# First rows loaded as bf16 over the hardware queues, weight columns ahead, and normalisation scalars read directly, in a two-layer transformer kernel

## The chip, the cores and the metric

The kernel runs on one core of a Trainium2 chip. The metric is device time in microseconds (us): the median of several executions. Experiments of one group ran on the same chip, in turns with the kernel before.

The engines are PE (matmuls), ACT (activation functions), DVE (elementwise work), POOL (slower elementwise work and one kind of DMA) and SP (issues DMAs). Each engine works through its own instruction list.

## The reference

Two rounds of attention and a gated MLP, with the same weights in both rounds. S = 2048 rows, D = 512, 32 heads of 16, F = 1792, all bf16.

```python
def _layernorm(x, axis=-1, eps=1e-5):
    m = jnp.mean(x, axis=axis, keepdims=True)
    v = jnp.var(x, axis=axis, keepdims=True)
    return (x - m) / jnp.sqrt(v + eps)
...
    x = A_x
    x = x + _A_ref(_layernorm(x, axis=-1), A_wqkv, A_wo)
    x = x + _B_ref(_layernorm(x, axis=-1), B_w_gate, B_w_up, B_w_down)
    x = x + _A_ref(_layernorm(x, axis=-1), A_wqkv, A_wo)
    x = x + _B_ref(_layernorm(x, axis=-1), B_w_gate, B_w_up, B_w_down)
```

`_A_ref` is softmax attention over all 2048 keys, and `_B_ref` is `(gelu(x@wg) * (x@wu)) @ wd`.

## The kernel before

Rows are handled in four blocks of 512 rows. The "head" is the start of the program: X is loaded, normalised and transposed to XNT block by block, and K, Q and V are projected from XNT. Attention works in units (four heads for one block of queries). A unit makes score groups on PE, exponentials on ACT (some on DVE), and P·V on PE. After the eight units of a query block, a "post" runs beside the next block's attention: output projection, normalisation, MLP, normalisation.

The order on each engine is fixed when the program is generated. The generator keeps a clock of its own, gives every operation an assumed cost, and always emits what it believes to be ready next. The last number of each operation below is that assumed cost in us.

```python
    def ln_scale(n, then):
        ...
        job("pool", 1, [
            (lambda e: e.tensor_scalar(LNS[:, 0, 0:n], var, LN_EPS, None, op0=ALU.add), mvk, [("LNS",)], 0.3),
            (lambda e: e.tensor_tensor(LNS[:, 1, 0:n], LNS[:, 0, 0:n], CM05[:, 0:n], op=ALU.pow),
             [("LNS",), ("CM05",)], [("LNS",)], 1.1),
            (lambda e: e.tensor_scalar(LNS[:, 2, 0:n], mean, -1.0, None, op0=ALU.mult), mvk + [("LNS",)], [("LNS",)],
             0.3)], then)

    def ln_apply(i, xs_, eng, alt, then=None):
        job(eng, 1, [(lambda e: e.tensor_scalar(xn(i, alt), X[:, xs_, :], LNS[:, 2, i:i + 1], LNS[:, 1, i:i + 1],
                                                op0=ALU.add, op1=ALU.mult),
                      [("X", xs_), ("LNS",)], [xnkey(i, alt)], 1.05 if eng == "pool" else 0.46)], then)
...
    def post(layer, qb):            # cut
        ...
        yield from ln_thread(tts, xsl, True, (layer, qb, 2), "dve" if qb == NQB - 1 else "pool")
        ...                          # MLP, cut
        if not last:
            yield from ln_thread(tts, xsl, True, (layer, qb, 1), "dve" if qb == NQB - 1 else "pool")
```

PE takes "keep-clock" matmuls (zeros added to the accumulator, L1253) when it would otherwise idle. They are meant to keep its clock up.

## Time and profile before

| | before |
|---|---|
| time, median of 3 | 1768.59 us |
| ACT busy | 1602 us, 91% |
| PE busy (keep-clock included) | 1614 us, 91% |
| DVE busy | 1276 us, 72% |
| POOL busy | 208 us, 12% |

The timeline of ACT in the first 100 us of the kernel before. Columns: start, busy us, engine, line, operation, out<-in, count, and in brackets the idle time before and what ended it. Instructions that follow each other are merged.

```profile
0.79 1.28 ACT L561 ACT_TABLE_LOAD   x1 [0.79 <-PEq L2260]
18.56 0.60 ACT L561 ACTIVATE fXNT<-fPS 128x512 bf16<-128x512 bf16 x1 [16.49 <-PE fPS L552]
...
30.78 6.82 ACT L1128 ACTIVATE fPT<-fPS 128x1536 bf16<-128x1536 f32 x5 [9.03 <-PE fPS L1123]
50.14 6.86 ACT L1128 ACTIVATE fPT<-fPS 128x1536 bf16<-128x1536 f32 x5 [12.54 <-PE fPS L1123]
60.92 8.16 ACT L1128 ACTIVATE fPT<-fPS 128x1536 bf16<-128x1536 f32 x6 [3.92 <-PE fPS L1123]
74.96 25.64 ACT L1128 ACTIVATE fPT<-fPS 128x1536 bf16<-128x1536 f32 x26 [5.87 <-PE fPS L1123]
```

The first exponentials start at 30.8 us. They come in bursts of five or six, because unit 0 needs the K of each further key block. From 75 us on ACT runs without long gaps. Of PE's 1614 us, 257 us are keep-clock matmuls, so ACT is the engine with the most real work, and its idle time before 75 us is what a faster head can recover.

The normalisation applies in the same kernel (query by source line: minimum, median and maximum duration in ns, first and last start):

```profile
L545 POOL TENSOR_SCALAR fHT<-fX,fLNS x36: 768/772/777, 294.9 to 1548.7; 128x512 bf16<-128x512 f32 x36
L545 DVE TENSOR_SCALAR fHT<-fX,fLNS x28: 528/541/3620, 14.2 to 1720.9; 128x512 bf16<-128x512 f32 x28
```

### The profile page before, as it was taken

The numbers are of one execution on the slowest core, as the hardware profiler recorded it, in microseconds if no ns is written. First come the engines' busy times: TensorE is split into PE (matmuls) and PEld (weight loads), VectorE is DVE, ScalarE is ACT, GpSimd is POOL, SyncE is SP. The second block draws the span as 40 slices with busy tenths as digits, with TensorE's granted clock in tenths as the row PEclk, the third lists the DMA queues.
The fourth block names the chain that finished last, engine by engine and source line by source line (L and its number), as shares of the span: only waits on it lengthen the run. The fifth ranks groups of instructions, "written<-read, shape, count | busy, mean of one in ns | idle before, by whom it ended". The sixth has DMA issues, their size and how long they took to land.

```text
span 1766.0 us, 38383 instructions
## 1 busy us (share of the span) xinstructions
PE 1614.0 (91%) x16180; PEld 497.5 (28%) x16349; DVE 1276.4 (72%) x2103; ACT 1602.1 (91%) x1488; POOL 208.2 (12%) x226
## 2 busy tenths in 40 slices
PE   7898989999899999989999989999989899999998
PEld 3422222222222222332333322222222222222233
DVE  5799996577856878538653799767895588856853
ACT  2699889999999999999899999999999999999932
POOL 2502011011110011010330110201011000101000
PEclk9999999999999999999999999999999999999999
DMA  5200000143111530125214100013401142012513
GB/s 156 73 2 17 2 15 10 47 119 115 41 37 41 162 86 17 43 57 158 65 48 133 41 18 9 17 49 102 148 18 31 51 134 91 23 39 81 152 27 104
DMA packets 138705, 114.00 MB, mean 65 GB/s; under 512 B 12320, under 2 KB 126240, under 8 KB 138528
## 3 DMA queue, kind: packets, MB, share of 16 engines
q1 hardware_dynamic: 134256, 103.07, 20.3%
q0 software_dynamic: 4272, 8.39, 1.7%
q8 instruction: 133, 2.18, 0.5%
q14 instruction: 44, 0.36, 0.1%
HBM read 97.78 MB, written 6.82 MB: 59 GB/s over the span
## 4 chain that ended last, share of the span: by engine, by line
ACT 61%; PE 21%; DVE 14%; issue 1%; POOL 1%; DMA 1%; SPq 0%; DVEq 0%; POOLq 0%
ACT fPT L1128 58%; DVE fPI L1162 6%; PE fPS L575 6%; PE fPS L1123 5%; DVE fPP L1184 5%; PE fPS L1233 4%; PE fPS L1253 3%; ACT fHT L1094 2%; PE fPS L932 2%; DVE fQ L618 1%; PE fPS L638 1%; DVE fHT L545 1%; ACT L1094 1%; DMA fX<-in_A_x_dram 0%; POOL fVD L651 0%
## 5 line engine op out<-in xcount | busy, mean ns | idle before, releaser
L1128 ACT ACTIVATE fPT<-fPS 128x1024 bf16<-128x1024 f32 (+1 forms) x1440 | 1527.4, 1212 | 83.1 <-PE fPS L1123 81.1
L1123 PE MATMUL fPS<-fQ,fKT 32*128 32x512 bf16 x4096 | 554.2, 385 | 71.5 <-ACT fPT L1128 56.0
L1162 DVE TENSOR_SCALAR fPI<-fPS 128x512 int16<-128x512 f32 x768 | 504.3, 683 | 65.5 <-PE fPS L1123 63.9
L1233 PE MATMUL fPS<-fPT,fVP 128*17 128x512 bf16 x3328 | 432.9, 384 | 13.1 <-ACT fPT L1128 6.7
L1184 DVE TENSOR_SCALAR fPP<-fPI 128x2048 int16<-128x2048 int16 x576 | 393.7, 716 | 4.4 <-PE fPS L1233 3.4
L1123 PEld LDWEIGHTS fPS<-fQ,fKT 32*128 32x128 bf16 x4096 | 138.8, 91 | 617.3 <-ACT fPT L1128 527.1
L1233 PE MATMUL fPS<-fPP,fVD 128*17 128x512 f16 x2304 | 302.3, 381 | 6.4 <-DVE fPP L1184 6.1
L1253 PE MATMUL fPS<-fONB,fZV 128*17 128x512 bf16 x3356 | 256.6, 386 | 5.0 <-POOL fONB L344 4.1
L575 PE MATMUL fPS<-fXNT,fWR 128*128 128x512 bf16 x831 | 212.9, 381 | 20.3 <-DVE fHT L918 8.9
L1233 PE MATMUL fPS<-fPI,fVP 128*17 128x512 f16 x768 | 217.4, 384 | 0.5 <-DVE fPP L1184 0.5
L918 DVE TENSOR_TENSOR fHT<-fPS,fHT 128x512 bf16<-128x512 f32 x112 | 77.0, 689 | 140.0 <-PE fPS L575 92.4
L1233 PEld LDWEIGHTS fPS<-fPT,fVP 128*17 128x17 f16 x3328 | 100.0, 87 | 177.4 <-issue 127.2
L767 POOL TENSOR_TENSOR fAT<-fOS,fRB 128x512 bf16<-128x512 f32 x32 | 42.6, 1330 | 830.1 <-DMA fRB<-rscr 784.8
L895 DVE CAST fHT<-fPS 128x512 bf16<-128x512 f32 x98 | 67.5, 689 | 85.4 <-PE fPS L575 85.3
L932 PE MATMUL fPS<-fWR,fHT 128*128 128x512 bf16 x407 | 115.4, 382 | 6.5 <-issue 4.8
L575 PEld LDWEIGHTS fPS<-fXNT,fWR 128*128 128x128 bf16 x896 | 71.9, 97 | 123.2 <-DVE fHT L918 21.6
L1253 PEld LDWEIGHTS fPS<-fONB,fZV 128*17 128x17 f16 x3356 | 77.0, 91 | 84.5 <-issue 40.7
L1233 PEld LDWEIGHTS fPS<-fPP,fVD 128*17 128x17 f16 x2304 | 69.8, 88 | 88.8 <-issue 48.0
L651 POOL TENSOR_SCALAR fVD<-fVP 128x544 f16<-128x544 f16 (+1 forms) x48 | 53.9, 1124 | 130.5 <-DVE fVP L659 127.8
L808 DVE COPY fOS<-fPS 128x512 f32<-128x512 f32 x64 | 43.8, 684 | 23.8 <-PE fPS L1233 23.7
L533 POOL TENSOR_SCALAR fLNS<-fMV 128x4 f32<-128x4 f32 x16 | 6.3, 395 | 460.3 <-DVE fMV L526 460.2
L1233 PEld LDWEIGHTS fPS<-fPI,fVP 128*17 128x17 f16 x768 | 47.4, 88 | 34.2 <-issue 19.3
(60 smaller groups left out, 693.8 us busy)
## 6 DMA issues: line engine op xcount, KB each, us to landing
fWR<-in_B_w_down_dram SPq DMA_DIRECT2D x189, 256.0 KB, 3.0
fWR<-in_B_w_gate_dram SPq DMA_DIRECT2D x56, 256.0 KB, 3.3
fWR<-in_B_w_up_dram SPq DMA_DIRECT2D x56, 256.0 KB, 2.9
fRB<-rscr SPq DMA_DIRECT2D x256, 32.0 KB, 1.8
fX<-in_A_x_dram POOLq DMA_DIRECT2D x7, 1024.0 KB, 5.4
xscr<-fX SPq DMA_DIRECT2D x16, 256.0 KB, 2.1
fX<-xscr SPq DMA_DIRECT2D x4, 1024.0 KB, 6.2
fAT<-fATS SPq DMA_DIRECT2D x128, 16.0 KB, 1.8
```

The source lines that it names most:

```text
L575: ins = e.matmul(bank(bs[0])[:, 0:cols], lhsT=l, rhs=r_, start=(i == 0), stop=(i == n - 1))
L651: job("pool", 2, [(lambda e, dst=dst, src=src, ph=ph: e.tensor_scalar(dst, src, 2.0 ** (-ph / NPH), None, op0=ALU.mult), [("VP", c, k) for ...
L895: evac_job(1, b, [(lambda e: e.tensor_copy(HT[:, ft, :], bank(b)), [BK[b]], [("HT", ft)], 0.6)], got(("gate", layer, qb, ft)))
L918: (lambda e: e.tensor_tensor(HT[:, ft, :], bank(b), HT[:, ft, :], op=ALU.mult), [BK[b], ("HT", ft)], [("HT", ft)], 0.62)], got(("up", laye ...
L932: ins = e.matmul(bank(b)[:, 0:D], lhsT=HT[:, ft, i * 128:(i + 1) * 128], rhs=WR[:, s, jj * D:(jj + 1) * D], start=(ft == 0), stop=(ft == N ...
L1094: sch.op("act", lambda e, lo=lo, hi=hi: e.activation(HT[:, lo:hi, :], HT[:, lo:hi, :], ACTF.Gelu_apprx_tanh), r=keys, w=keys, cost=0.05 + ...
L1123: ins = e.matmul(bank(b0 + k), lhsT=KT[32 * j:32 * j + 32, c, kt * 128:(kt + 1) * 128], rhs=Q[32 * j:32 * j + 32, qs, :], start=True, stop ...
L1128: o = sch.op("act", lambda e: e.activation(PT[:, p, 0:512 * na].rearrange("p (a b) -> p a b", a=na), PS[:, b0:b0 + na, :], ACTF.Exp, scale ...
L1162: dve(0, [(lambda e: e.tensor_scalar(PI[:, gi, 512 * r:512 * (r + 1)], bank(b0 + n - 1), DBIAS, 0.0, op0=ALU.add, op1=ALU.max), [bks[-1]], ...
L1184: shifts.append((s, [(lambda e: e.tensor_scalar(PP[:, s, :], PI[:, gi, :], int(OCT) * ph // NPH, None, op0=ALU.add), [("PI", gi, r) for r ...
L1233: ins = e.matmul(PS[32 * j:32 * j + VW, ACC, :], lhsT=l, rhs=r_, start=a, stop=z, tile_position=(0, 32 * j), skip_group_check=True)
L1253: ins = e.matmul(PS[32 * j:32 * j + VW, ACC, :], lhsT=ZV[:, :], rhs=ones, start=False, stop=False, tile_position=(0, 32 * j), skip_group_c ...
```

## The change

Its intent is to shorten the head:

- X arrives as bf16, without a cast, over the hardware queues into the space of the f32 residual ring, all 16 tiles at once.
- The first 128 columns of each QKV weight come ahead on the ACT queue.
- Start-up memsets move from POOL to DVE.
- Block 0's scale operations run in pairs, half of its copies into XNT move from ACT to DVE, and its Q projections come before its V projections.
- The statistics of blocks 1 to 3 get the priority of the K, Q and V evictions (copies of results out of PSUM, the matmul accumulator) instead of standing behind them.
- The negation of the mean (one small POOL operation per normalisation) is dropped. The apply now subtracts the mean itself.

```diff
-    for t in range(4):
-        dma("pool", "ldx0_%d" % t, X[:, t, :], x_in[0, 128 * t:128 * (t + 1), :], w=[("X", t)], kb=256)
-    dma("sp", "ldw_k", WK[:], wq_src[:, :, D:2 * D], w=[("WK",)], kb=512)
-    ...                                                        # the same for WQ, WV
+    for t in range(4):
+        dma("sp", "ldx0_%d" % t, xb(t), x_in[0, 128 * t:128 * (t + 1), :], w=[("XB", t)], kb=128)
+    W3 = (("WK", WK, D), ("WQ", WQ, 0), ("WV", WV, 2 * D))
+    for name, W, lo in W3:
+        dma("act", "ld0" + name, W[:, :, 0:128], wq_src[:, :, lo:lo + 128], w=[(name, 0)], kb=128)
+    ...                                                        # blocks 1 to 3 of X and the other columns, on sp
     def ln_scale(n, then, lo=0):
         ...
-            (lambda e: e.tensor_scalar(LNS[:, 2, 0:n], mean, -1.0, None, op0=ALU.mult), ...
-    def ln_apply(i, xs_, eng, alt, then=None):
-        job(eng, 1, [(lambda e: e.tensor_scalar(xn(i, alt), X[:, xs_, :], LNS[:, 2, i:i + 1], LNS[:, 1, i:i + 1],
-                                                op0=ALU.add, op1=ALU.mult),
+    def ln_apply(i, rows, key, eng, alt, then=None, us=None):
+        us = us or (1.05 if eng == "pool" else 0.46)
+        job(eng, 1, [(lambda e: e.tensor_scalar(xn(i, alt), rows, MV[:, i, 0:1], LNS[:, 1, i:i + 1],
+                                                op0=ALU.subtract, op1=ALU.mult),
     ...
-        for i, x in enumerate(xset(b)):
-            stats(i, x, got(("st", name, i)), prio=0 if b == 0 else 2)
+        for i, tt in enumerate(tts):
+            stats(i, xb(tt), ("XB", tt), got(("st", name, i)), prio=0 if b == 0 else 1)
```

`ln_scale` and `ln_apply` are helpers. The head uses them, and so do the post stages.

More of the change, by code (lines that the diff above doesn't have):

```diff
@@ L333, in pool, with xb @@
         return o
+    def xb(tt):
+        return X[:, tt // 2, :].bitcast(BF)[:, D * (tt % 2):D * (tt % 2) + D]
     wq_src = wqkv.rearrange("(a p) n -> p a n", p=128)
     for t in range(4):
-        dma("pool", "ldx0_%d" % t, X[:, t, :], x_in[0, 128 * t:128 * (t + 1), :], w=[("X", t)], kb=256)
-    dma("sp", "ldw_k", WK[:], wq_src[:, :, D:2 * D], w=[("WK",)], kb=512)
-    dma("sp", "ldw_q", WQ[:], wq_src[:, :, 0:D], w=[("WQ",)], kb=512)
-    dma("sp", "ldw_v", WV[:], wq_src[:, :, 2 * D:3 * D], w=[("WV",)], kb=512)
+        dma("sp", "ldx0_%d" % t, xb(t), x_in[0, 128 * t:128 * (t + 1), :], w=[("XB", t)], kb=128)
+    W3 = (("WK", WK, D), ("WQ", WQ, 0), ("WV", WV, 2 * D))
+    for name, W, lo in W3:
+        dma("act", "ld0" + name, W[:, :, 0:128], wq_src[:, :, lo:lo + 128], w=[(name, 0)], kb=128)
+    for b in range(1, NQB):
+        dma("sp", "ldx%d" % b, X[:, 2 * b:2 * b + 2, :].bitcast(BF).rearrange("p a (c d) -> p (a c) d", c=2),
+            x_in[0, 512 * b:512 * b + 512, :].rearrange("(a p) c -> p a c", p=128),
+            w=[("XB", 4 * b + i) for i in range(4)], kb=512)
+        if b == 1 and NCK > 1:
+            for name, W, lo in W3:
+                dma("sp", "ld1" + name, W[:, :, 128:D], wq_src[:, :, lo + 128:lo + D],
+                    w=[(name, c) for c in range(1, NCK)], kb=384)
     sch.op("pool", lambda e: e.memset(CM05[:], -0.5), w=[("CM05",)])
@@ L353, in _emit_fast @@
            r=[("QMASK",)], w=[("QMASK",)])
-    sch.op("dve", lambda e: e.memset(PS[:, ACC, :], 0.0), w=[BK[ACC]])
-    dma("sp", "ldw_o", WO[:], wo.rearrange("(a p) n -> p a n", p=128), w=[("WO",)], kb=512)
-    def late_init():
-        sch.op("pool", lambda e: e.memset(AP(VP, 16, [[NKT * H * VW, 128], [VW, NKT * H]]), 1.0), w=[("VPONE",)])
-        sch.op("pool", lambda e: e.memset(RB[:], 0.0), w=[("RB", i, j) for i in range(NRB) for j in range(4)])
-        sch.op("pool", lambda e: e.memset(OKL[:], 1.0), w=[("OKL",)])
-        sch.op("pool", lambda e: e.memset(OKV[:], 1.0), w=[("OKV",)])
-        sch.op("pool", lambda e: e.memset(LT[:], 1.0), w=[("LT", i) for i in range(HB)])
+    sch.op("dve", lambda e: e.memset(PS[:, ACC, :], 0.0), w=[BK[ACC]], cost=0.6)
+    sch.op("dve", lambda e: e.memset(AP(VP, 16, [[NKT * H * VW, 128], [VW, NKT * H]]), 1.0), w=[("VPONE",)], cost=0.6)
+    sch.op("dve", lambda e: e.memset(RB[:], 0.0), w=[("RB", i, j) for i in range(NRB) for j in range(4)], cost=0.6)
+    sch.op("dve", lambda e: e.memset(OKL[:], 1.0), w=[("OKL",)])
+    sch.op("dve", lambda e: e.memset(OKV[:], 1.0), w=[("OKV",)])
+    sch.op("dve", lambda e: e.memset(LT[:], 1.0), w=[("LT", i) for i in range(HB)])
+    dma("sp", "ldw_o", WO[:], wo.rearrange("(a p) n -> p a n", p=128), w=[("WO",)], kb=512)
     wg_src = wg.rearrange("(a p) n -> p a n", p=128)
@@ L522, in xnkey, with stats, ln_scale @@
         return ("HT", i + 4 * alt)
-    def stats(i, xs_, then=None, prio=1):
-        dve(prio, [(lambda e: e.bn_stats(ST[:, i, :], X[:, xs_, :]), [("X", xs_)], [("ST", i)], 0.72),
+    def stats(i, rows, key, then=None, prio=1):
+        dve(prio, [(lambda e: e.bn_stats(ST[:, i, :], rows), [key], [("ST", i)], 0.72),
                    (lambda e: e.bn_aggr(MV[:, i, :], ST[:, i, :]), [("ST", i)], [("MV", i)], 0.1)], then)
-    def ln_scale(n, then):
-        mvk = [("MV", i) for i in range(n)]
-        mean = AP(MV, 0, [[8, 128], [2, n]])
-        var = AP(MV, 1, [[8, 128], [2, n]])
+    def ln_scale(n, then, lo=0):
+        keys = [("MV", lo + i) for i in range(n)]
+        var = AP(MV, 2 * lo + 1, [[8, 128], [2, n]])
         job("pool", 1, [
-            (lambda e: e.tensor_scalar(LNS[:, 0, 0:n], var, LN_EPS, None, op0=ALU.add), mvk, [("LNS",)], 0.3),
-            (lambda e: e.tensor_tensor(LNS[:, 1, 0:n], LNS[:, 0, 0:n], CM05[:, 0:n], op=ALU.pow),
-             [("LNS",), ("CM05",)], [("LNS",)], 1.1),
-            (lambda e: e.tensor_scalar(LNS[:, 2, 0:n], mean, -1.0, None, op0=ALU.mult), mvk + [("LNS",)], [("LNS",)],
-             0.3)], then)
+            (lambda e: e.tensor_scalar(LNS[:, 0, lo:lo + n], var, LN_EPS, None, op0=ALU.add), keys,
+             [("LNS", lo + i) for i in range(n)], 0.3),
+            (lambda e: e.tensor_tensor(LNS[:, 1, lo:lo + n], LNS[:, 0, lo:lo + n], CM05[:, 0:n], op=ALU.pow),
+             [("LNS", lo + i) for i in range(n)] + [("CM05",)], [("LNS", lo + i) for i in range(n)], 1.1)], then)
     def ln_check(n):
@@ L542, in ln_check @@
                  [("MV", i) for i in range(n)] + [("OKV",)], [("OKV",)], 0.1)])
-    def ln_apply(i, xs_, eng, alt, then=None):
-        job(eng, 1, [(lambda e: e.tensor_scalar(xn(i, alt), X[:, xs_, :], LNS[:, 2, i:i + 1], LNS[:, 1, i:i + 1],
-                                                op0=ALU.add, op1=ALU.mult),
-                      [("X", xs_), ("LNS",)], [xnkey(i, alt)], 1.05 if eng == "pool" else 0.46)], then)
+    def ln_apply(i, rows, key, eng, alt, then=None, us=None):
+        us = us or (1.05 if eng == "pool" else 0.46)
+        job(eng, 1, [(lambda e: e.tensor_scalar(xn(i, alt), rows, MV[:, i, 0:1], LNS[:, 1, i:i + 1],
+                                                op0=ALU.subtract, op1=ALU.mult),
+                      [key, ("MV", i), ("LNS", i)], [xnkey(i, alt)], us)], then, ported=True)
     def transpose_piece(i, tt, alt=False, eng="dve", then=None):
@@ L587, in _emit_fast @@
     xloaded = set()
-    xhere = {0}
+    xhere = set()
     def xset(n):
@@ L593, in xload @@
     def xload(n):
-        layer, qb = (n - NQB) // NQB if n >= NQB else 0, n % NQB
-        if n in xloaded or n >= NQB + n_rep * NQB or layer and ("xs", layer, qb) not in have:
+        layer, qb = n // NQB, n % NQB
+        if n in xloaded or n >= n_rep * NQB or layer and ("xs", layer, qb) not in have:
             return
@@ L606, in issue @@
                            x_in[0, rows, :].rearrange("(a p) c -> p a c", p=128),
-                           w=[("X", x) for x in sl], serial=True, kb=1024)
-            job("pool", 3, [(issue, [], [("X", x) for x in sl], None)], lambda o: xhere.add(n))
+                           w=keys, serial=True, kb=1024)
+            keys = [("X", x) for x in sl] + [("XB", 2 * x + i) for x in sl for i in range(2) if 2 * x + i < NTT]
+            job("pool", 3, [(issue, [], keys, None)], lambda o: xhere.add(n))
     def qproj(layer, up):
@@ L622, in qproj @@
         return mm_piece([(WQ[:, ck, 128 * c:128 * (c + 1)], XNT[:, ck, 512 * qb:512 * (qb + 1)]) for ck in range(NCK)],
-                        xk(qb) + [("WQ",)], evac)
+                        xk(qb) + [("WQ", c)], evac)
     def kproj(layer, c, kb):
         return mm_piece([(WK[:, ck, 128 * c:128 * (c + 1)], XNT[:, ck, 512 * kb:512 * (kb + 1)]) for ck in range(NCK)],
-                        xk(kb) + [("WK",)],
+                        xk(kb) + [("WK", c)],
                         lambda b: evac_job(1, b, [(lambda e: e.tensor_copy(KT[:, c, 512 * kb:512 * (kb + 1)], bank(b)),
@@ L662, in after @@
                              [BK[b]], [("VP", c, kb)], 0.6)], then)
-        return Piece(0.064 * 4 * NCK, xk(kb) + [("WV",)], fn, after)
+        return Piece(0.064 * 4 * NCK, xk(kb) + [("WV", c)], fn, after)
     units_done = [0] * n_rep
@@ L680, in kv @@
             add(gate, lambda: kproj(layer, c, b))
+            if b == 0 and c in cl:
+                q(c)
             add(gate, lambda: vproj(layer, c, b))
@@ L692, in prep_list @@
                 kv(c, b)
-                if b == 0:
-                    q(c)
         for b in range(NQB):
@@ L857, in ln_thread @@
         for i, tt in enumerate(tts):
-            ln_apply(i, xsl[i], eng, False, got(("xn", name, i)))
+            ln_apply(i, X[:, xsl[i], :], ("X", xsl[i]), eng, False, got(("xn", name, i)))
         for i, tt in enumerate(tts):
@@ L870, in post @@
         tts = [4 * qb + i for i in range(4)]
-        n_ = NQB + layer * NQB + qb
+        n_ = layer * NQB + qb
         xsl = xset(n_)
@@ L879, in evac_x @@
                                  [BK[b], ("X", x)], [("X", x)], 0.62)],
-                         lambda o: stats(i, x, got(("st", (layer, qb, 2), i))))
+                         lambda o: stats(i, X[:, x, :], ("X", x), got(("st", (layer, qb, 2), i))))
             yield mm_piece([(AT[:, c, i * 128:(i + 1) * 128], WO[:, c, :]) for c in range(NCK)],
@@ L959, in keep @@
                              got(("xs", layer + 1, qb)) if i == 3 else None, kb=256)
-                        stats(i, x, got(("st", (layer, qb, 1), i)))
+                        stats(i, X[:, x, :], ("X", x), got(("st", (layer, qb, 1), i)))
                     evac_job(1, b, [(lambda e, b=b, x=x: e.tensor_tensor(X[:, x, :], bank(b)[:, 0:D], X[:, x, :],
@@ L1269, in head_source @@
                 yield None
-        if b:
-            while b not in xhere:
-                yield None
-        for i, x in enumerate(xset(b)):
-            stats(i, x, got(("st", name, i)), prio=0 if b == 0 else 2)
-        while not all(("st", name, i) in have for i in range(4)):
-            yield None
-        ln_scale(4, got(("lns", name)))
-        while ("lns", name) not in have:
-            yield None
-        for i, x in enumerate(xset(b)):
-            ln_apply(i, x, "dve", alt, got(("xn", name, i)))
-        if b == 0:
-            late_init()
+        parts = [(0, 2), (2, 2)] if b == 0 else [(0, 4)]
+        for i, tt in enumerate(tts):
+            stats(i, xb(tt), ("XB", tt), got(("st", name, i)), prio=0 if b == 0 else 1)
+        for lo, n in parts:
+            while not all(("st", name, i) in have for i in range(lo, lo + n)):
+                yield None
+            ln_scale(n, got(("lns", name, lo)), lo)
+            while ("lns", name, lo) not in have:
+                yield None
+            for i in range(lo, lo + n):
+                ln_apply(i, xb(tts[i]), ("XB", tts[i]), "dve", alt, got(("xn", name, i)), us=0.2)
         for i, tt in enumerate(tts):
@@ L1286, in head_source @@
                 yield None
-            yield transpose_piece(i, tt, alt=alt, eng="act" if b == 0 else "dve", then=got(("tr", name, i)))
-        xload(b + 2)
+            yield transpose_piece(i, tt, alt=alt, eng="act" if b == 0 and i % 2 == 0 else "dve", then=got(("tr", name, i)))
         while not all(("tr", name, i) in have for i in range(4)):
@@ L1291, in head_source @@
         have.add(("xnt", 0, b))
+        if b == NQB - 1:
+            xload(0)
+            xload(1)
     def heads():
@@ L1295, in heads @@
             yield from head_source(b)
-    if NQB > 1:
-        xload(1)
     for layer in range(n_rep):
```

## The prediction

> **What bounds the kernel now.** The page gives ACT 91% busy (1602 us), PE 91%, DVE 72%; the chain that ended last is ACT exp (L1128) for 58% of the span. Time is saved only where ACT stops idling. Table by stage: ACT is over 90% busy nearly everywhere after 75 us, except the last 72. In 0-75 us it does 17 exp slots (1.37 us each, 23 us), the XNT copies and a table load; about 49 us are idle. The change touches that head.
>
> **Why the head is slow** (timeline). SWDGE X tiles land 7-11 us in; statistics end 12.4; scales on POOL 1.6 us; the four applies take 4.98 us beside POOL's VP/RB memsets (1.92 us when clean); XNT of block 0 ends 21.8; first exp 30.8. Unit 0 waits for each block's K: exps of blocks 1, 2, 3 start at 50.1, 60.9, 75.0, after waits of 12.5, 3.9, 5.9 us. The block cadence (12-19 us) comes from late statistics (block 1 at 38.3, its X long landed: instruction order), POOL's VD scalings (4.9 us) ahead of block 3's scales, and slow applies.
>
> **What changes.**
> - X arrives as bf16, 128 KB per tile, hardware queue first: I expect landing at 3-4.5 us instead of 7-11.5. The Trainium skill, "DMA: Bandwidth & Descriptors", Specifications, gives about 0.6 us to first byte on that path against about 1 us on the gpsimd path; the WK load took 4.0 us for 512 KB here.
> - First-head weight columns: 256 B runs, but only 384 KB, needed near 10 us. No loss.
> - Five memsets move from POOL (4 us) to DVE: estimate 2-2.5 us, ending near 3.5.
> - Statistics stay 0.68+0.18 us per tile. Applies from bf16: 0.54 us becomes about 0.25 us (estimate; "VectorE: DVE Perf Modes", Mode 4x_2P: four elements per cycle).
> - The mean negation (0.24 us) goes, and block 0's scales come in pairs.
> - Later blocks' statistics get the priority of K/V evictions, so they come first.
>
> **Estimate.** Block 0: statistics end 7, XNT 10.5; then block 1's statistics (3.3 us) run ahead of K and Q evictions (0.7+1.4 us): first exp near 16. Cadence per block, DVE-limited: statistics 3.3, applies 1, copies 1.5, two evictions 1.4, some other chunks' evictions: 7.5-10 us, against 7.3 us of exps per block. Block 3's first exp near 40 us instead of 75.0, with ACT almost filled from 16 on. Gross gain 35 us. Given back: about 12 evictions (8 us DVE, 10 us PE) that ran in the idle head move to 75-300 us, where DVE and ACT are both about 95% busy and PE's keep-clock matmuls (about 27 us of real slack) are the reserve: 2-6 us. A reshuffled static order adds several us either way. Net about 30 us.
>
> **Predicted: 1738 us, 8 in 10 within 1722-1753.** Faster by over 2% (below about 1733): 0.32; within 2%: 0.67; slower: 0.01.
>
> **What would show it.** Timeline: X landing before 5 us; first exp at 14-19 us; exps of block 3 starting 36-47 us; bf16 applies 0.2-0.3 us. Table by stage: ACT idle in 0-75 us down from 49 to about 16-22; exp counts after the head unchanged; 75-300 us with fewer keep-clock matmuls and slightly more ACT idle or longer exps. Tail unchanged.
>
> **What would make it wrong.** Evictions of other chunks queuing ahead of applies, cadence 12 us: then only 20 us gain. Conversely, a cadence of 7 us and free deferred evictions: 38 us. Also a worse static order in a later stage; 256 B runs delaying X; applies not speeding up.

## More of the kernel before

The post normalisations of query blocks 0 to 2 apply the scalars on POOL. That makes six stages in layer 0 and three in layer 1, so nine stages of four applies. In the head, and for the last block, DVE applies them.

## The result, and the profile after

The kernel after took 1776.41 us (median of 4, 1776.02 to 1777.38), against 1769.59 us for the kernel before in the same comparison. A ratio here is the mean time of one kernel's fast runs over that of the other's of the same rounds, so it is not quite the ratio of the medians quoted beside it. This one is 1.0038, with a 95% interval of 1.0018 to 1.0059. The kernel became slightly slower (by less than 2%), where 30 us of gain had been predicted.

The same ACT timeline, kernel after:

```profile
21.82 13.54 ACT L1139 ACTIVATE fPT<-fPS 128x1536 bf16<-128x1536 f32 x10 [9.39 <-PE fPS L1134]
40.92 8.16 ACT L1139 ACTIVATE fPT<-fPS 128x1536 bf16<-128x1536 f32 x6 [5.57 <-PE fPS L1134]
50.10 32.91 ACT L1139 ACTIVATE fPT<-fPS 128x1536 bf16<-128x1536 f32 x32 [1.01 <-PE fPS L1134]
```

The head did what it was meant to do. As before, 16 exponentials precede the steady stretch, but that stretch now begins at 50.1 us instead of 75.0. At that point the kernel is 24.9 us ahead. It therefore loses some 32 us later (24.9 plus the 7 by which it ends up behind). The applies, kernel after:

```profile
L555 POOL TENSOR_SCALAR fHT<-fX,fMV,fLNS x36: 2072/2081/2611, 263.5 to 1554.0; 128x512 bf16<-128x512 f32 x36
L555 DVE TENSOR_SCALAR fHT<-fX,fMV,fLNS x28: 381/410/546, 8.1 to 1729.0; 128x512 bf16<-128x512 bf16 x16, 128x512 bf16<-128x512 f32 x12
```

The f32 applies on DVE alone, as a group (busy us, mean ns, idle before):

```profile
L555 DVE TENSOR_SCALAR fHT<-fX,fMV,fLNS 128x512 bf16<-128x512 f32 x12 | 5.7, 541 | 3.4 <-POOL fLNS L545 3.4
```

This is the surprise. The same 36 applies on POOL, of the same shape and types, went from 772 to 2081 ns. On DVE an f32 apply kept its 541 ns. POOL as a whole is busy only 14% of the span, so the page's first table hides this. But the nine stages feed PE, which turns the applied rows. The first of them, on PE, kernel after (timeline, 128x128 matmuls of L562 are the transposes of the applied rows):

```profile
265.77 0.38 PE L562 MATMUL fPS<-fIDN,fHT 128*128 128x128 bf16 x4 [0.50 <-POOL fHT L555]
...
267.84 0.38 PE L562 MATMUL fPS<-fIDN,fHT 128*128 128x128 bf16 x4 [0.82 <-POOL fHT L555]
268.15 0.40 PE L1244 MATMUL fPS<-fPT,fVP 128*17 128x512 bf16 x4
269.90 0.59 PE L562 MATMUL fPS<-fIDN,fHT 128*128 128x128 bf16 x4 [1.35 <-POOL fHT L555]
270.42 0.61 PE L1134 MATMUL fPS<-fQ,fKT 32*128 32x512 bf16 x3
270.96 0.61 PE L1264 MATMUL fPS<-fONB,fZV 128*17 128x512 bf16 x4
271.96 0.59 PE L562 MATMUL fPS<-fIDN,fHT 128*128 128x128 bf16 x4 [0.39 <-POOL fHT L555]
```

PE waits for each of the four rows in turn, and the score matmuls (L1134) stand behind the transposes although they need nothing from POOL. From 269.9 to 275.9 us, the same matmul groups take about 0.6 us instead of 0.4: PE's clock has dropped. The table by stage shows it (PEclk is the granted clock, here 1.00, 0.50 and 1.00):

```profile
core 0: us, PE busy (x) PEld busy (x) DVE busy (x) ACT busy (x) POOL busy (x), PEclk, DMA share, GB/s
266.00:269.30 3.30, 1.73 (x22) 0.55 (x19) 0.85 (x2) 2.86 (x3) 3.30 (x2) 1.00 0.00 0
269.30:276.10 6.80, 5.81 (x33) 1.75 (x33) 1.47 (x3) 2.97 (x3) 2.51 (x2) 0.50 0.00 0
276.10:280.00 3.90, 3.84 (x29) 1.10 (x25) 1.44 (x3) 3.67 (x3) 0.00 (x0) 1.00 0.22 64
```

The Trainium skill, "TensorE: Matmul & The Clock Gate", Part 1, says that the clock falls to half after one idle window of about 3.4 us. The trace agrees about the half, but PE was not idle for so long at a stretch: its longest wait was 1.35 us, and in the 3.3 us before the drop it was busy for 1.73 us.

ACT had run this stage (from 295 us on) without a gap in the kernel before:

```profile
283.60 32.00 ACT L1128 ACTIVATE fPT<-fPS 128x1536 bf16<-128x1536 f32 x25
```

In the kernel after, it starves:

```profile
260.69 8.16 ACT L1139 ACTIVATE fPT<-fPS 128x1536 bf16<-128x1536 f32 x6 [0.28 <-PE fPS L1134]
271.07 1.45 ACT L1139 ACTIVATE fPT<-fPS 128x1536 bf16<-128x1536 f32 x1 [2.22 <-PE fPS L1134]
273.13 1.45 ACT L1139 ACTIVATE fPT<-fPS 128x1536 bf16<-128x1536 f32 x1 [0.61 <-PE fPS L1134]
276.04 1.45 ACT L1139 ACTIVATE fPT<-fPS 128x1536 bf16<-128x1536 f32 x1 [1.45 <-PE fPS L1134]
277.72 5.97 ACT L1139 ACTIVATE fPT<-fPS 128x1536 bf16<-128x1536 f32 x5 [0.23 <-PE fPS L1134]
```

The gaps shown add up to 4.8 us in this one of the nine stages. What the others cost is shown in experiment 1.

### The profile page after: what moved, and what is told of

Same layout as the page of the kernel before. It is cut to its first block, busy times and chain, and to the rows that moved or that the text cites. A ratio compares the mean times of both kernels' runs of the same rounds, so it can differ in the third digit from the quotient of the medians.

```text
span 1774.4 us, 38110 instructions
## 1 busy us (share of the span) xinstructions
PE 1643.3 (93%) x16129; PEld 495.7 (28%) x16129; DVE 1272.6 (72%) x2117; ACT 1605.2 (90%) x1486; POOL 243.1 (14%) x200
## 4 chain that ended last, share of the span: by engine, by line
ACT 54%; PE 28%; DVE 11%; POOL 4%; issue 1%; DMA 1%; SPq 0%; POOLq 0%; DVEq 0%
ACT fPT L1139 50%; PE fPS L585 8%; PE fPS L1134 7%; PE fPS L1244 5%; DVE fPI L1173 5%; DVE fPP L1195 3%; POOL fHT L555 3%; PE fPS L943 3%; PE fPS L1264 3%; ACT fHT L1105 2%; DVE fQ L629 1%; PE fPS L649 1%; PE fPS L562 1%; POOL fLNS L545 1%; ACT L1105 1%
## 5 line engine op out<-in xcount | busy, mean ns | idle before, releaser
L1134 PE MATMUL fPS<-fQ,fKT 32*128 32x512 bf16 x4096 | 557.3, 388 | 69.3 <-ACT fPT L1139 54.0
L1244 PE MATMUL fPS<-fPT,fVP 128*17 128x512 bf16 x3324 | 437.8, 388 | 3.8 <-DVE fPP L1195 2.0
L1134 PEld LDWEIGHTS fPS<-fQ,fKT 32*128 32x128 bf16 x4096 | 139.6, 91 | 612.8 <-ACT fPT L1139 508.3
L1244 PE MATMUL fPS<-fPP,fVD 128*17 128x512 f16 x2316 | 297.7, 383 | 8.3 <-DVE fPP L1195 7.5
L1264 PE MATMUL fPS<-fONB,fZV 128*17 128x512 bf16 x3124 | 243.6, 389 | 2.4 <-POOL fQMASK L361 1.5
L585 PE MATMUL fPS<-fXNT,fWR 128*128 128x512 bf16 x896 | 232.2, 388 | 11.9 <-DVE fHT L929 9.0
L943 PE MATMUL fPS<-fWR,fHT 128*128 128x512 bf16 x448 | 123.6, 383 | 0.4
L1264 PEld LDWEIGHTS fPS<-fONB,fZV 128*17 128x17 f16 x3124 | 72.2, 91 | 75.8 <-issue 33.0
L555 POOL TENSOR_SCALAR fHT<-fX,fMV,fLNS 128x512 bf16<-128x512 f32 x36 | 75.3, 2106 | 0.9
L576 DVE COPY fXNT<-fPS 128x512 bf16<-128x512 bf16 x62 | 25.2, 422 | 61.9 <-PE fPS L562 61.7
L543 POOL TENSOR_SCALAR fLNS<-fMV 128x4 f32<-128x4 f32 (+1 forms) x17 | 7.6, 444 | 451.3 <-DVE fMV L537 451.3
```

Of the source, the lines that this page charges most:

```text
L555: job(eng, 1, [(lambda e: e.tensor_scalar(xn(i, alt), rows, MV[:, i, 0:1], LNS[:, 1, i:i + 1], op0=ALU.subtract, op1=ALU.mult), [key, ("MV ...
L585: ins = e.matmul(bank(bs[0])[:, 0:cols], lhsT=l, rhs=r_, start=(i == 0), stop=(i == n - 1))
L943: ins = e.matmul(bank(b)[:, 0:D], lhsT=HT[:, ft, i * 128:(i + 1) * 128], rhs=WR[:, s, jj * D:(jj + 1) * D], start=(ft == 0), stop=(ft == N ...
L1134: ins = e.matmul(bank(b0 + k), lhsT=KT[32 * j:32 * j + 32, c, kt * 128:(kt + 1) * 128], rhs=Q[32 * j:32 * j + 32, qs, :], start=True, stop ...
L1244: ins = e.matmul(PS[32 * j:32 * j + VW, ACC, :], lhsT=l, rhs=r_, start=a, stop=z, tile_position=(0, 32 * j), skip_group_check=True)
L1264: ins = e.matmul(PS[32 * j:32 * j + VW, ACC, :], lhsT=ZV[:, :], rhs=ones, start=False, stop=False, tile_position=(0, 32 * j), skip_group_c ...
```

## The experiments

Several variants exceed a limit on the relative error that appears to be 0.02, by millionths. The variants fall on either side without a pattern in what they change, so this is a knife edge of the arithmetic as a whole.

### 1. One word changed, the order of all instructions identical

Theory 1 is that the subtract form is slow on POOL and the in-order lists wait for it. Theory 2 is that the earlier head reshuffled the whole static order for the worse. Theory 3 is that the cost comes from the two scalars lying in different tensors. The change had altered the operation and the tensor of the scalar together. The following two kernels separate the two. In the traces, their instruction order is that of their parents on every engine. (In one trace some PE matmul records are missing. There it is the same for the weight loads.)

```diff
# a_add: the kernel after (wrong result on purpose)
-                                                op0=ALU.subtract, op1=ALU.mult),
+                                                op0=ALU.add, op1=ALU.mult),
# b_sub: the kernel before (wrong result on purpose)
-                                                op0=ALU.add, op1=ALU.mult),
+                                                op0=ALU.subtract, op1=ALU.mult),
```

> The kernel after, with one word changed: the apply adds the mean instead of subtracting it (a slightly wrong result on purpose). The order of instructions is identical on every engine. Theory 1 (the subtract form is slow on POOL: 2081 ns against 772 ns, and the in-order schedule waits for it): the 36 POOL applies fall to about 0.77 us and the time to about 1742 us (1734 to 1752). Theory 2 (the later stages are slower because the whole static order was reshuffled by the earlier head): applies fall, time stays within 1768 to 1778. Theory 3 (POOL is slow because its two scalar operands now lie in two different tensors): applies stay at 2.08 us and the time at 1776.

> The kernel before, with one word changed: subtract instead of add in the apply, both scalars from one tensor as before (wrong sign of the mean on purpose, same order of instructions). Theory 1: POOL applies rise from 0.77 to 2.08 us and the time by 25 to 40 us, to about 1800. Theory 2: applies rise, time within 1 per cent of before, below 1782. Theory 3: applies stay at 0.77 us, time 1769.

Measured: a_add 1739.05 us, ratio to before 0.983 (0.981 to 0.985). b_sub 1800.52 us, ratio 1.0182 (1.0165 to 1.0199), against 1769.55 us for the kernel before. The relative error is 0.646 for both. Their outputs are wrong, which doesn't matter for the times. Groups of instructions on POOL, first a_add, then b_sub (busy us, mean ns, idle before):

```profile
L555 POOL TENSOR_SCALAR fHT<-fX,fMV,fLNS 128x512 bf16<-128x512 f32 x36 | 28.0, 789 | 0.9
```

```profile
L545 POOL TENSOR_SCALAR fHT<-fX,fLNS 128x512 bf16<-128x512 f32 x36 | 74.5, 2076 | 0.9
```

With two tensors and add it is fast, with one tensor and subtract slow. Theory 3 is out. With the order untouched, the word is worth about 37 us in the kernel after (1.0038 minus 0.983, times 1769) and 31 to 32 us in the kernel before. Theory 2 is out as the cause of the loss. The mean granted clock of the profiled runs goes along: 0.996 for a_add, 0.982 for b_sub and for the kernel after. ACT in a_add, the stage shown above:

```profile
259.12 18.07 ACT L1139 ACTIVATE fPT<-fPS 128x1536 bf16<-128x1536 f32 x14 [0.28 <-PE fPS L1134]
277.46 3.77 ACT L1139 ACTIVATE fPT<-fPS 128x1024 bf16<-128x1024 f32 x4 [0.28 <-PE fPS L1134]
```

The starving is gone. What PE waited for in the whole run, kernel after and then a_add (us in total, times, longest):

```profile
PE fPS L562 <- POOL fHT L555: 22.1, 27, 1.6
```

```profile
PE fPS L562 <- POOL fHT L555: 0.2, 1, 0.2
```

Since the order is the same, the start times of ACT's exponentials in the two traces can be compared one by one. At the last of them the kernel after is 34 us behind a_add. Seven of the nine stages cost it 3.6 to 5.6 us each, 33 us in all. In each of these seven, PE waits 2.4 to 3.5 us for the applies and its clock then falls to half for 6.8 to 10.2 us. In the stage at 688 us PE waits 1.6 us, the clock stays up, and 0.9 us are lost. In the one at 845 us PE doesn't wait, and nothing is lost. In b_sub the same seven stages cost 2.6 to 6.9 us each and the other two nothing.

36 applies times 1.3 us is 47 us of added POOL time, and 31 to 37 us of it reached the end, from an engine that is 14% busy.

### 2. Two ways to repair it

```diff
# a_neg: the kernel after; nine POOL normalisations negate the mean again and add
+            (lambda e: e.tensor_scalar(LNS[:, 2, lo:lo + n], AP(MV, 2 * lo, [[8, 128], [2, n]]), -1.0, None, op0=ALU.mult), ... 0.3)   # if neg
-        ... MV[:, i, 0:1], LNS[:, 1, i:i + 1], op0=ALU.subtract, op1=ALU.mult),
+        ... LNS[:, 2, i:i + 1] if eng == "pool" else MV[:, i, 0:1], LNS[:, 1, i:i + 1],
+            op0=ALU.add if eng == "pool" else ALU.subtract, op1=ALU.mult),
# a_dve: the kernel after; all applies on DVE
-        yield from ln_thread(tts, xsl, True, (layer, qb, 2), "dve" if qb == NQB - 1 else "pool")
+        yield from ln_thread(tts, xsl, True, (layer, qb, 2), "dve")         # and the same for (layer, qb, 1)
```

> The kernel after, correct, with the negated mean (0.24 us on POOL) and add given back to the nine POOL normalisations only; the head keeps the subtract on DVE. Theory 1: POOL applies 0.77 us, time 1735 to 1750, that is 1.1 to 1.9 per cent faster than before. Theory 2: 1768 or more. The static order differs a little from the one after, since the model counts the extra 0.3 us.

> The kernel after, all applies on DVE (0.41 to 0.54 us each), subtract kept. Theory 1: no PE wait for slow POOL applies, time 1738 to 1755 with about 19 us more DVE work spread over nine stages. Theory 2: near 1770, as any other order.

Measured: a_neg 1737.48 us, ratio 0.9821 (0.9805 to 0.9838), relative error 0.020001. a_dve 1731.00 us, ratio 0.9783 (0.9767 to 0.9800), relative error 0.020002. The expectation for a_neg held. a_dve came out 7 us below its range: moving 19.5 us of applies to DVE costs nothing that shows. It is also 6.5 us faster than a_neg, with POOL's fast form. But the two have different orders, and order alone can move the time by nearly 5 us (experiment 5), so it is not shown that DVE is the better place.

### 3. Slow operation or wrong order?

Is a 2.08 us apply bad in itself, or only because the order was made for 1.05 us?

```diff
# a_cost: the kernel after, subtract still on POOL; only the generator's assumption changes
-        us = us or (1.05 if eng == "pool" else 0.46)
+        us = us or (2.1 if eng == "pool" else 0.46)
```

> The kernel after, subtract still on POOL at 2.08 us, but the generator that fixes the order now reckons with 2.1 us for a POOL apply instead of 1.05, so it can place other matmuls before the transposes that wait for it. If most of the 37 us that a_add won back were in-order waiting behind a late transpose, this wins back well over half: 1740 to 1758. If they were a true dependency (the attention of later blocks or the MLP cannot start earlier), it stays near 1770 to 1778.

Measured: 1740.47 us against 1768.78, ratio 0.9839 (0.9822 to 0.9855), relative error 0.020006. One number, which never reaches the chip, wins back nearly everything. POOL is still slow, but the applies no longer hold PE up: its waits for POOL's L555 are gone from the trace. The gain of 36 us is far more than the nearly 5 us by which orders alone differ in experiment 5. The same stage of a_cost, POOL first, then PE, then ACT:

```profile
263.21 8.27 POOL L555 TENSOR_SCALAR fHT<-fX,fMV,fLNS 128x512 bf16<-128x512 f32 x4
```

```profile
266.22 0.40 PE L562 MATMUL fPS<-fIDN,fHT 128*128 128x128 bf16 x4
...
267.56 0.61 PE L1264 MATMUL fPS<-fONB,fZV 128*17 128x512 bf16 x8
268.10 0.40 PE L562 MATMUL fPS<-fIDN,fHT 128*128 128x128 bf16 x4
268.58 0.39 PE L1134 MATMUL fPS<-fQ,fKT 32*128 32x512 bf16 x3
...
270.25 0.40 PE L562 MATMUL fPS<-fIDN,fHT 128*128 128x128 bf16 x4
```

```profile
260.36 30.02 ACT L1139 ACTIVATE fPT<-fPS 128x1536 bf16<-128x1536 f32 x23 [0.27 <-PE fPS L1134]
```

POOL takes the same 8.27 us for its four applies. PE reaches each transpose only after its row has arrived, and has done scores and keep-clock matmuls in between. Its groups stay at 0.4 us, and ACT runs 30 us without a gap. The loss in the kernel after was therefore in-order waiting behind a transpose placed too early, together with the clock drop that the waiting brought. It was not a dependency that had to be paid. How much of the 37 us is the wait and how much the slower clock was not separated by a run. The traces bound both: the waits for POOL's L555 are 22 us, and the mean granted clocks (0.982 over 1774 us against 0.996 over 1738 us) come to at most 25 us of lost PE time, an estimate. So neither alone makes up the loss.

### 4. The head: why its gain was 25 us and not 35

```diff
# a_dve_p2: a_dve; statistics of blocks 1 to 3 behind the evictions again
-            stats(i, xb(tt), ("XB", tt), got(("st", name, i)), prio=0 if b == 0 else 1)
+            stats(i, xb(tt), ("XB", tt), got(("st", name, i)), prio=0 if b == 0 else 2)
# a_dve_bk: a_dve; PSUM banks 0 to 2 kept for the first scores
         pool_ = set(free_banks)
+        if slot_no[0] < 1:
+            pool_ -= {0, 1, 2}
```

> a_dve with the statistics of blocks 1 to 3 put back behind the K, Q and V evictions, as before the change. The prediction named this priority as what delays the first exps. Expected if so: first exp at about 18 us instead of 22, later blocks up to 3 us later each, block 3 exps near 50; time 1726 to 1736. If the order of these does not matter: within 2 us of a_dve, 1729 to 1733.

> a_dve with PSUM banks 0 to 2 kept free for the first score group, so that the first scores need not wait for projections to give their banks back. Expected if banks hold up the first exp: first exp at 18 to 19 us instead of 22, block 3 exps start 1 to 4 us earlier than 50.4, time 1726 to 1731. Rival (the cadence of the four blocks, not the first exp, sets the end of the head): first exp earlier, block 3 exps still near 50, time unchanged within 2 us.

> The kernel after unchanged, to see its own relative error beside that of a_neg and a_dve, which exceed 0.02 by one millionth. Expected: the same error of 0.0200 within a few millionths, since the arithmetic of the normalisation is the same; time 1776.

Measured: a_dve_p2 1741.31 us, ratio 0.9835 (0.9814 to 0.9857), correct. a_dve_bk 1730.91 us, ratio 0.9787 (0.9771 to 0.9803), relative error 0.020003. a_copy, the unchanged kernel after, 1773.86 us in a single execution of unknown state, correct. The ACT timelines, a_dve_p2 first, then a_dve_bk:

```profile
15.43 1.45 ACT L1139 ACTIVATE fPT<-fPS 128x1536 bf16<-128x1536 f32 x1 [3.40 <-PE fPS L1134]
...
54.41 26.56 ACT L1139 ACTIVATE fPT<-fPS 128x1536 bf16<-128x1536 f32 x27 [8.52 <-PE fPS L1134]
```

```profile
17.09 1.45 ACT L1141 ACTIVATE fPT<-fPS 128x1536 bf16<-128x1536 f32 x1 [4.98 <-PE fPS L1136]
18.94 5.48 ACT L1141 ACTIVATE fPT<-fPS 128x1536 bf16<-128x1536 f32 x4 [0.40 <-PE fPS L1136]
27.84 6.82 ACT L1141 ACTIVATE fPT<-fPS 128x1536 bf16<-128x1536 f32 x5 [3.42 <-PE fPS L1136]
40.09 8.16 ACT L1141 ACTIVATE fPT<-fPS 128x1536 bf16<-128x1536 f32 x6 [5.43 <-PE fPS L1136]
49.53 31.08 ACT L1141 ACTIVATE fPT<-fPS 128x1536 bf16<-128x1536 f32 x30 [1.28 <-PE fPS L1136]
```

(a_dve itself ran on another chip. The ratios, each to the kernel before on the same chip, are what compares.) Both kernels have their first exponentials five to seven us earlier than the 22.1 us of a_dve, and neither is faster. In a_dve_bk blocks follow each other after 10.8, 12.3 and 9.4 us, and block 3 starts at 49.5 us against 50.4 in a_dve. The cadence of the four blocks sets the end of the head, as the rival expectation for a_dve_bk said. a_dve_p2 missed both of its expected ranges: the later statistics push block 3 to 54.4 us, where about 50 was expected. Of its 10 us loss, 4 are visible there. It also shows a granted clock of 0.90 to 0.93 between 130 and 250 us, where a_dve has 1.00; over the whole run its four executions have 0.983 to 0.989, against 0.993 to 0.995. Why that order drops the clock was not pursued. The new priority of the statistics thus helps the head by 4 us; whether the other 6 belong to it is not shown.

### 5. Three more draws

```diff
# a_dve_pipe: a_dve; ST, MV, LNS twice as large, block b + 1's statistics queued (priority 2) with block b's scales
+            if lo + n == 4 and b + 1 < NQB:
+                head_stats(b + 1, 2)
# a_dve_pipe_bk: the same, with the bank reservation of a_dve_bk
# a_dve_whole: a_dve; Q, K, V weights whole on the first queue after block 0 of X
-        dma("act", "ld0" + name, W[:, :, 0:128], wq_src[:, :, lo:lo + 128], w=[(name, 0)], kb=128)
+        dma("sp", "ld0" + name, W[:], wq_src[:, :, lo:lo + D], w=[(name, c) for c in range(NCK)], kb=512)
```

> a_dve with the statistics of the next block computed ahead, in the gaps that DVE has while the present block is transposed (double the small statistics tiles, lowest priority). Theory: the block cadence of 9 to 12 us in a_dve is a serial chain in which 3.3 us of statistics wait for the block before. Expected if so: exps of block 3 start at 42 to 46 us instead of 50.4 and the time falls by 3 to 7 us to 1724 to 1728. Rival (cadence set by PE order and other evictions, or the gain is used up by evictions that move into the full stage): block 3 near 50, or time within 2 us of 1731.

> a_dve_pipe with banks 0 to 2 kept for the first scores too. By a_dve_bk, which moved the first exp by 5 us and the time not at all, expected within 2 us of a_dve_pipe. It is also a second draw of the static order, to see how much the order alone moves the time and the relative error (0.0200 plus or minus millionths).

> a_dve with the Q, K, V weights loaded whole on the first queue after block 0 of X, as before the change, instead of the first 128 columns ahead on the ACT queue. If the first columns ahead matter: the first K projection waits for its 512 KB, several us later than 12.6 us, and block 3 exps after 52 us, time 1733 to 1740. If X alone was the limit: first projection at 12 to 13 us as in a_dve, time within 3 us of 1731.

Measured: a_dve_pipe 1734.65 us, ratio 0.9814 (0.9797 to 0.9830), correct. a_dve_pipe_bk 1739.44 us, ratio 0.9833 (0.9815 to 0.9850), correct. a_dve_whole 1736.66 us, ratio 0.9822 (0.9805 to 0.9838), relative error 0.020001; the kernel before took 1768.20 us beside them.

- a_dve_pipe missed its expectation. Block 3's exponentials start at 50.0 us, as in a_dve, so its rival expectation held and nothing was won. What sets the cadence beyond the statistics remains open.
- a_dve_pipe_bk has the same head to within 0.01 us and is nearly 5 us slower. Only the order of the rest differs, so order alone can move the time by this much. The slower one has the lower granted clock (0.987 to 0.991 against 0.991 to 0.995 in four executions each). Differences of this size are not explained here.
- In a_dve_whole the first K projection starts at 13.0 us, against 12.6 in the kernel after, so the weights did not hold it up. That part of the expectation failed. The loss appears later: ACT waits 12.5 us for block 1, whose exponentials start at 35.3 us. The 1.5 MB of weights now ahead of it on the queue are not what held it: block 1's X landed at 11.9 us (8.6 in a_dve), but its statistics start only at 18.2 us, behind block 0's evictions in the order. Block 3 starts at 55.1 us, and the time is 5.7 us above a_dve's. Both lie in the expected range, but by another route.

The fastest correct version, a_dve_pipe, is 1.9% faster than before and faster than the kernel after. a_dve and a_dve_bk are 2.1 to 2.2% faster, but miss the error limit by 2 to 3 millionths.

## Why the prediction was right or wrong

The predicted 1738 us (1722 to 1753) missed, since 1776 us was measured. Point by point:

- **"The change touches that head": wrong, and this is the step that failed.** The dropped negation sits in a helper that nine post stages use too. The prediction counted it as a saving of 0.24 us ("The mean negation (0.24 us) goes") and looked up the new apply only on DVE. The form that came in its place costs 2081 ns instead of 772 on POOL, 36 times, and the order was made for 1.05 us. a_add and b_sub, with nothing else altered, put this at 37 and 31 to 32 us. "Exp counts after the head unchanged" was true of ACT (1440 in all, before and after), and it hid the loss.
- **The net gain of the rest, "about 30 us": right.** a_neg, the change with the add given back to POOL, is 32 us faster than before (1737.48 against 1769.55), and the predicted figure was 1738. Its parts were not as predicted, however, so that the sum agrees is partly luck. The head gave 24.9 us and not 35. The 2 to 6 us to be given back don't show at the end: compared with the kernel before, exponential by exponential, a_neg is 25 us ahead at 75 us, 29 ahead after the first POOL stage and 30 at the last. What brought the additional gain is not shown.
- **First exponentials near 16 us: 21.8 measured.** Block 0's four X tiles landed at 3.3 to 6.6 us (3 to 4.5 expected, 7.1 to 11.5 before), its statistics ended at 8.2 us instead of 7, and its XNT was done at 12.5 us instead of 10.5. These times contain the whole transfer; the first-byte times that the prediction cites from the skill are not seen apart in any run here. The first scores were then placed behind block 1's transposes. a_dve_bk showed that this cost nothing in the end.
- **Block cadence 7.5 to 10 us, block 3 near 40 us: 50.1 us measured for block 3, and a cadence of 9 to 12 us in a_dve_bk, where all blocks can be told apart.** The named danger, evictions of other chunks ahead of the applies, is visible on DVE between 15.6 and 18.7 us, but a_dve_pipe shows that taking the statistics out of the chain doesn't cure it.
- **Applies from bf16 at about 0.25 us: 0.41 us measured.** Under "VectorE: DVE Perf Modes", The TRN2 errata, the Trainium skill puts the measured fixed term near 150 cycles. With four elements per cycle that gives an estimate of (150 + 128) / 0.96 GHz = 0.29 us, still below the trace.
- **256-byte weight runs harmless: right** as far as the first projection goes. a_dve_whole, without them, is 5.7 us slower, but through its order, as experiment 5 says.

## What to carry to other kernels

Before changing the form of an operation in a shared helper, list every engine and stage that uses the helper, and take the duration of the new form on each of those engines from a trace. An engine that is 12% busy can hold up the whole program where another engine's in-order list waits for it, so judge it by what waits on it, not by its share. Where the order is generated from assumed costs, compare those costs with the trace after each change. Here, correcting one of them was worth nearly as much as removing the slow operation (1740.5 against 1737.5 us).

## What the Trainium skill lacked or had wrong

- "GPSIMD Engine Reference", section 3.1, gives about 1.8 cycles per element at best for a simple loop, 768 ns predicted for 512 elements. The add-then-multiply form agrees with 772 ns. The page doesn't say that another first operation can cost far more: subtract-then-multiply of the same shape took 2081 ns, 4.9 cycles per element at the page's 1.2 GHz. Section 4.1's remark that one-input operations run at roughly line rate doesn't hold for it.
- "VectorE: DVE Perf Modes", The TRN2 errata: the estimate from its fixed term of about 150 cycles is 0.29 us for a 512-element bf16 apply with two per-partition scalars. The trace shows 0.41 us (0.54 us from f32). Whether the fixed term or the four elements per cycle is off is not shown: with two per cycle the same estimate is 0.42 us.
- "TensorE: Matmul & The Clock Gate" tells of the clock falling after an idle window of about 3.4 us, and of kernels in which short idle times make it fall, without a figure for these. The runs add one: waits of 0.50, 0.82 and 1.35 us within 4.6 us, after which the groups of matmuls take 0.6 us instead of 0.4, and half clock for 6.8 us.
- No page has the cost of batch statistics on DVE: 0.66 us per 128x512 tile from bf16 and 0.685 us from f32, so the narrower type hardly helps there.
